# A decode step of attention and SwiGLU on one core: the output in two column tiles, the chain ahead of W_O on two engines, W_O in five pieces

## The chip, the cores and the metric

The kernel runs on one core of one Trainium2 chip. The metric is the device time of one execution in microseconds, on the slowest core, which here is the only one. Five engines work side by side, each with its own program: TensorE (PE in the profile) for matmuls, VectorE (DVE), ScalarE (ACT), GpSimd (POOL) and SyncE (SP), which mostly issues DMAs. They wait for each other on semaphores. Matmuls write into PSUM, and DVE and ACT read it from there.

## The reference

One new token for each of four sequences (B = 4, D = 512). The normed input goes through grouped-query attention over the last 4096 positions of a cache (32 query heads, 8 key/value heads of 128), and beside it through a SwiGLU feed-forward of width 1792. Cut to what matters:

```python
xn = layernorm(x)                                   # (4, 1, 512)
q  = xn @ wq                                        # 32 heads of 128
p  = softmax(q . k[:, :, Sk-4096:] * 128 ** -0.5)   # k, v: 8 heads, each for 4 query heads
a  = concat_heads(p . v) @ wo                       # wo: 4096 x 512
f  = (silu(xn @ w_gate) * (xn @ w_up)) @ w_down     # 1792 wide
return x + a + f
```

All inputs and the output are bf16. The windows of the two caches are 32 MB each, the weights another 13 MB.

## The kernel before, in words

**Loads.** SP (`on_sync`) issues nearly all loads, in one order: Wq, W_gate, W_up, then for each key/value head g = 0 to 7 the whole K of that head (4 MB, into `KB[g % 2]`) and the whole V (4 MB, into `VB[g % 2]`), then W_down, then W_O. The K load of head g waits until the transposes of head g-2 are done (L242), the V load until the products with V of head g-2 are done (L253). W_O goes into the buffer of K of head 6, so it waits for that head's transposes (L265). It comes in four pieces of 22, 5, 3 and 2 rows of 1 KB per partition (`WOS`); W_O's 4096 rows of 512 lie as 32 rows `e` on 128 partitions, and each piece has its own semaphore. At the end SP stores the left half of the output.

**One group per head** (the loop at L500, two heads a turn because of the two buffers). K arrives with positions on partitions and must be transposed: 16 chunks `c` of 8 transposes (`transposes`, L417), three PSUM banks `ps_kt` in turn. Each chunk is evicted into `KT`, by ACT for the chunks in `ACT_CH` (L281) and by DVE for the others (L330). Two chunks later `scores` (L432) multiplies them with the queries into four banks `ps_S`. DVE takes maxima (L336), PE and DVE turn them into one shift per query (L338 to L345), PE adds the shift (L444), ACT takes the exponential (L284) and `pv` (L453) multiplies by V into the left half of `ps_O`; sums of the exponentials (L459) go into the right half of the same bank. DVE then copies the left half to `Osb` (L348) and sums the right half into `dsum` (L349), one after the other. `fin` (L466, L468), run inside the next head's loop after its third chunk, finishes both sums, and DVE's `norm` (L353 to L358) divides and writes `OT`. `warm` puts matmuls of no use (`spin`, L474) into gaps of PE: five before the maxima, five before the shift, and four after `pv` of each even head from head 2 on.

**The end.** After the last head: `fin`, `down` (the feed-forward's last product, 14 matmuls into `acc4_ps`, L478), four small matmuls that bring `OT` into the order that W_O wants (L524, into one bank `perm_ps`), one DVE copy into `OP` (L374). Then PE takes W_O's pieces as they land. The first `WOE` = 22 rows go through `acc4`: 512 columns wide, one row `e` on each of four column tiles of 32 in turn, so that four partial sums stand in `acc4_ps`. ACT copies these to `S2` (L292), and a product with `sel4` adds them up. That product is in PE's program behind the second piece. The remaining rows go through `acc`: four matmuls per row, one for each 128 output columns, each on a column tile of its own, into `acc_ps`. So the four quarters of the output stand on four groups of partitions. DVE copies two of them into `y` (L377), ACT the other two (L295), SP stores the left half (L269) and ACT the right half (L298), and SP waits for both.

Of the kernel before, what the change touches and what calls it, by code (L numbers as in the profile page):

```python
# [10 lines left out]
def bass_parallel_sum__sliding_block_cached__swiglu_ffn__decode_kernel(  # L11
# [25 lines left out]
    NT = W // NJ  # L37
# [6 lines left out]
    SCALE = float(Dh) ** -0.5  # L44
    EPS = 1e-5
    OFF = -1.0e9
    WOS = (0, 22, 27, 30, 32)
    WOE = 22
    NR = HQ * Dh // 128

    def sb(name, shape, dtype, align=32):
# [65 lines left out]
    O_ps = ps_O[:, 0:2 * Dh]  # L117
    O2_ps = ps_S[3][:, 0:NH]
    D2_ps = ps_S[3][:, 64:64 + NH]
    den_ps = ps_O[:, 256:512]  # L120
    DT = 256 // NH
    q_ps = ps_S[0][:, 0:HQ * B]
    gate_ps = ps_O[:, 64:64 + NF * B]
    up_ps = ps_O[:, 128:128 + NF * B]
    xT_ps = ps_S[2][:, 0:NC * B]
    HD = D // 4
    acc_ps = ps_S[0][:, 0:HD]
    acc4_ps = ps_S[1]
    perm_ps = ps_kt[2][:, 0:B * NR]

    def sem(name):
        return nc.alloc_semaphore(name=name)
# [3 lines left out]
    d_wu = sem("d_wu")  # L136
    d_wd = sem("d_wd")
    d_out = sem("d_out")
    d_wo = [sem("d_wo%d" % q) for q in range(4)]
# [23 lines left out]
    s_p = sem("s_p")  # L163
    s_pv = sem("s_pv")
    s_dn = sem("s_dn")
    s_fin = sem("s_fin")
    s_nrm = sem("s_nrm")
    s_pm = sem("s_pm")
# [1 line left out]
    s_e = sem("s_e")  # L170
    s_ec = sem("s_ec")
    s_acc = sem("s_acc")
    s_y = [sem("s_y%d" % n) for n in range(2)]

    x_ap = A_x.rearrange("b s d -> (b s) d")
    out_ap = out.rearrange("b s (n c) -> n (b s) c", n=2)
# [61 lines left out]
    def on_sync(eng):  # L238
        def load(g):
            u = g % 2  # L240
            if g >= 2:
                eng.wait_ge(s_tr, NCH * (g - 1))  # L242
            if g < HKV - 1:
                eng.dma_start(KB[u][:], kv_ap(A_k_cache, g, 0, NT)).then_inc(d_k[u], 16)
            else:

                H = NT // 2
                eng.dma_start(KB[u][:, 0:H], kv_ap(A_k_cache, g, 0, H)).then_inc(d_k[u], 16)
                eng.dma_start(KB[u][:, H:], kv_ap(A_k_cache, g, H, NT)).then_inc(d_kh, 16)
            if g == 1:  # L250
                eng.wait_ge(s_q, 1)
            if g >= 2:
                eng.wait_ge(s_pv, g - 1)  # L253
            eng.dma_start(VB[u], kv_ap(A_v_cache, g, 0, NT)).then_inc(d_v[u], 16)

        def load_wo(n, a, b):
            eng.dma_start(WO[:, a:b, :], wo_ap[:, a:b, :]).then_inc(d_wo[n], 16)  # L257
# [11 lines left out]
        eng.dma_start(out_ap[0], y[:, 0:D // 2]).then_inc(d_out, 16)  # L269
        eng.wait_ge(d_out, 32)  # L270

    def on_scalar(eng):
        eng.wait_ge(s_go, 1)
        eng.dma_start(X[:], x_ap).then_inc(d_x, 16)
        eng.wait_ge(s_var, 1)
        eng.activation(st_std[:], st_var[:], ACT.Sqrt).then_inc(s_std, 1)

        def group(r):
            for n, c in enumerate(ACT_CH):
                eng.wait_ge(s_tr, r * NCH + (c + 1))  # L280
                eng.activation(KT[:, c % 4], kt_ps[c % 3], ACT.Copy).then_inc(s_ea, 1)  # L281
# [10 lines left out]
        eng.activation(S2[:], acc4_ps[:], ACT.Copy).then_inc(s_ec, 1)  # L292
        eng.wait_ge(s_acc, 1)
        for n in range(2, 4):
            last = eng.activation(y[:, HD * n:HD * (n + 1)], acc_ps[32 * n:32 * n + B, :], ACT.Copy)  # L295
        last.then_inc(s_y[1], 1)
        eng.wait_ge(s_y[1], 1)
        eng.dma_start(out_ap[1], y[:, D // 2:D]).then_inc(d_out, 16)  # L298

    def on_vector(eng):  # L300
        eng.wait_ge(d_x, 16)
# [24 lines left out]
        def group(r, rest=None):  # L326
            for c in range(NCH):
                if c not in ACT_CH:
                    eng.wait_ge(s_tr, r * NCH + (c + 1))
                    eng.tensor_copy(KT[:, c % 4], kt_ps[c % 3]).then_inc(s_ev, 1)  # L330
                if c == 2 and rest:
                    rest()
                for q in range(NB):
                    if c == min(NCH - 1, (q + 1) * NCH // NB + 1):
                        eng.wait_ge(s_sc, r * NB + (q + 1))
                        eng.tensor_reduce(mx[:, q, :], ps_S[q][:].rearrange("p (t n) -> p n t", n=NH), AX.X, ALU.max)  # L336
            eng.drain()
            eng.tensor_reduce(m16[:], mx[:].rearrange("p q n -> p n q"), AX.X, ALU.max).then_inc(s_m, 1)  # L338
            eng.tensor_copy(QC[:], QT[:, r + 1] if isinstance(r, int) else QT[:, bass.ds(r + 1, 1)].rearrange("p o n -> p (o n)"))
# [5 lines left out]
            eng.scalar_tensor_tensor(CM[0:NH, :], neg[:], M[:, 0:1], coff[:], ALU.mult, ALU.add).then_inc(s_cm, 1)  # L345

            eng.wait_ge(s_pv, r + 1)
            eng.tensor_copy(Osb[:], O_ps)  # L348
            eng.tensor_reduce(dsum[:], den_ps.rearrange("p (t n) -> p n t", n=NH), AX.X, ALU.add).then_inc(s_dn, 1)  # L349

        def norm(r):
# [19 lines left out]
            group(r, lambda: norm(r - 1))  # L371
        norm(HKV - 1)
        eng.wait_ge(s_pm, 1)
        eng.tensor_copy(OP[:, :, 0:B].rearrange("p r b -> p b r"), perm_ps.rearrange("p (b r) -> p b r", b=B)).then_inc(s_pc, 1)  # L374
        eng.wait_ge(s_acc, 1)
        for n in range(2):
            last = eng.tensor_copy(y[:, HD * n:HD * (n + 1)], acc_ps[32 * n:32 * n + B, :])  # L377
        last.then_inc(s_y[0], 1)

    def on_tensor(eng):  # L380
        mm = eng.matmul
# [22 lines left out]
        eng.sem_inc(s_p, NB)  # L404
        eng.sem_inc(s_nrm, 1)
        eng.sem_inc(s_dn, 1)
        eng.wait_ge(s_zero, 1)
        eng.wait_ge(s_guT, 1)

        def transposes(r, u, c):  # L410
            if c == 0:
                eng.wait_ge(d_k[u], (r - u) * 8 + 16)
            if u and c == NCH // 2:
                with eng.If(r > HKV - 2):
                    eng.wait_ge(d_kh, 16)
            for k in range(CH):
                last = eng.transpose(kt_ps[c % 3][:, k, :], KB[u][:, CH * c + k, :], ident[:])  # L417
            last.then_inc(s_tr, 1)
# [29 lines left out]
        def pv(r, u):  # L448
            for t in range(0, NT, 2):
# [6 lines left out]
                if t % DT == DT - 2:  # L456
                    e = t // DT
                    n = e % 4
                    last = mm(den_ps[32 * n:32 * n + 32, :], ones[:, 0:32],  # L459
                              P[:, DT * e:DT * (e + 1), :].rearrange("p t n -> p (t n)"),  # L460
                              start=False, stop=(e >= NT // DT - 4), skip_group_check=True)
            last.then_inc(s_pv, 1)

        def fin(r):
            eng.wait_ge(s_dn, r + 1)
            mm(D2_ps, head[:], dsum[:], start=True, stop=True, skip_group_check=True)  # L466
            for h in range(2):
                last = mm(O2_ps, Osb[:, Dh * h:Dh * (h + 1)], sel[:, NH * h:NH * (h + 1)],  # L468
                          start=(h == 0), stop=(h == 1), skip_group_check=True)
# [8 lines left out]
            return mm(acc4_ps[32 * n:32 * n + 32, :], left, right, start=start, stop=stop, skip_group_check=True)  # L478

        def acc(left, right, start, stop):  # L480
            for n in range(4):
                last = mm(acc_ps[32 * n:32 * n + B, :], left, right[:, HD * n:HD * (n + 1)],
                          start=start, stop=stop, skip_group_check=True)
            return last
# [4 lines left out]
            for t in range(NF):  # L489
                acc4(t % 4, guT[:, t, :], WD[:, t, :], t < 4, False)  # L490

        def warm(r, u, n):

            if u:
                spin(n)
            else:
                with eng.If(r > 0):
                    spin(n)

        with eng.Fori(0, HKV, 2) as r0:  # L500
            for u in range(2):
# [13 lines left out]
                eng.wait_ge(d_v[u], (r - u) * 8 + 16)  # L515
                pv(r, u)
                if u == 0:
                    warm(r, u, 4)

        fin(HKV)  # L520
        down()
        eng.wait_ge(s_nrm, HKV + 1)
        for b in range(B):
            last = mm(perm_ps[:, NR * b:NR * (b + 1)], OT[:, b].rearrange("p k h q -> p (k h q)"), dr[:])  # L524
# [4 lines left out]
        for q in range(4):  # L529
            eng.wait_ge(d_wo[q], 16)  # L530
            for e in range(WOS[q], WOS[q + 1]):
                if e < WOE:
# [45 lines left out]
```

## Time and profile before

| | us |
|---|---|
| time, median of 3 runs | 195.56 (195.43 to 195.69) |
| the profiled execution's own time | 195.57 |
| its span, first to last instruction | 194.2 |
| PE busy / DVE busy / ACT busy | 158.9 / 103.5 / 61.6 |
| mean granted clock of PE | 0.991 |

The profile's page gives busy times per engine, the span in 40 equal slices (one digit each, the busy tenths), the DMA queues, the chain of work that ended last, and the costliest groups of instructions: line, engine, operation, output <- inputs, shape, count, busy us, mean ns of one, and idle time before them. The other views used are the chain in order of time (start, us, what), the timeline (start, us, engine, line, operation) and a table by stretches of time: busy us and count of PE, PE's weight loads, DVE, ACT and POOL, then the granted clock of PE, the busy share of the 16 DMA engines and GB/s. Matmuls are pipelined and their ends are modelled, so their times overlap.

### The profile page before, as it was taken

The page shows a single profiled execution, that of the slowest core. Times are in us where ns is not written, and L with a number is a line of the kernel's source. Part 1 is how long each engine was busy: PE and PEld are TensorE (multiplying, and loading weights), DVE is VectorE, ACT ScalarE, POOL GpSimd, SP SyncE. Part 2 cuts the span into 40 slices and gives each one's busy share as a digit, 9 for nine tenths or more (in the row PEclk, how much of TensorE's full clock was granted, in tenths as well). Part 3 has the DMA queues.
Part 4 walks back from the last instruction along what each step waited for, and adds up shares of the span by engine and source line. Part 5 has one row for each costly group of instructions (what it writes and reads, how often), then busy time and mean ns, then how long its engine had stood idle before and what let it go on. Part 6 is the DMA issues. An engine that isn't in the chain of part 4 may idle for free.

```text
span 194.2 us, 7226 instructions
## 1 busy us (share of the span) xinstructions
PE 158.9 (82%) x3138; PEld 131.4 (68%) x3138; DVE 103.5 (53%) x218; ACT 61.6 (32%) x79; POOL 10.2 (5%) x49
## 2 busy tenths in 40 slices
PE   0009843998699899999999899989996999999964
PEld 0009843997388849966994699459945984897531
DVE  0071020368256837871886389338933893678241
ACT  1020000243405442624451345314531553063402
POOL 8750000000000000000000000000000000000000
PEclk9999999999789999999999999999999999999999
DMA  6999999999999999999999999999999999999992
GB/s 216 433 436 428 430 429 432 432 429 432 429 439 430 422 429 459 432 432 439 432 439 432 432 432 439 432 439 432 432 432 432 432 402 432 462 439 399 440 398 104
DMA packets 3634, 81.16 MB, mean 418 GB/s; under 512 B 412, under 2 KB 424, under 8 KB 808
## 3 DMA queue, kind: packets, MB, share of 16 engines
q1 hardware_dynamic: 3608, 81.01, 97.3%
q8 instruction: 8, 0.13, 0.2%
q14 instruction: 2, 0.02, 0.0%
q10 hardware_dynamic: 16, 0.01, 0.0%
HBM read 81.01 MB, written 0.00 MB: 417 GB/s over the span
## 4 chain that ended last, share of the span: by engine, by line
DMA 59%; PE 35%; DVE 3%; SPq 1%; issue 1%; DVEq 0%
DMA kbuf<-in_A_k_cache_dram 43%; PE ps_kt L417 21%; DMA kbuf<-in_A_wo_dram 16%; PE ps_s L432 7%; PE ps_o L453 3%; PE ps_s L468 1%; PE ps_kt L474 1%; PE ps_s L444 1%; DVE kT L330 1%; DVE mx L336 1%; SPq L257 1%; PE ps_s L466 1%; PE ps_o L459 0%; DVE y_sb L377 0%; PE ps_kt L439 0%
## 5 line engine op out<-in xcount | busy, mean ns | idle before, releaser
L417 PE MATMUL ps_kt<-ident,kbuf 128*128 128x128 bf16 x1024 | 78.4, 224 | 10.2 <-DMA kbuf<-in_A_k_cache_dram 9.8
L417 PEld LDWEIGHTS ps_kt<-ident,kbuf 128*128 128x128 bf16 x1024 | 60.7, 100 | 12.2 <-DMA kbuf<-in_A_k_cache_dram 10.9
L330 DVE COPY kT<-ps_kt 128x1024 bf16<-128x1024 bf16 x88 | 57.7, 686 | 20.4 <-PE ps_kt L417 19.6
L281 ACT ACTIVATE kT<-ps_kt 128x1024 bf16<-128x1024 bf16 x40 | 41.0, 1024 | 65.4 <-PE ps_kt L417 65.4
L432 PE MATMUL ps_s<-qC,kT 128*128 128x16 bf16 x1024 | 44.9, 170 | 2.9 <-DVE kT L330 2.0
L432 PEld LDWEIGHTS ps_s<-qC,kT 128*128 128x128 bf16 x1024 | 38.0, 97 | 4.8 <-DVE kT L330 4.0
L284 ACT ACTIVATE p<-ps_s 128x512 bf16<-128x512 f32 x32 | 16.5, 602 | 34.3 <-PE ps_s L444 34.3
L336 DVE TENSOR_REDUCE mx<-ps_s 128x16 f32<-128x512 f32 x32 | 22.0, 689 | 6.2 <-PE ps_s L432 4.2
L474 PE MATMUL ps_kt<-own,ones 128*128 128x512 bf16 x84 | 21.2, 380 | 0.0
L453 PE MATMUL ps_o<-vbuf,p 128*32 128x256 bf16 x512 | 19.2, 290 | 0.3
L453 PEld LDWEIGHTS ps_o<-vbuf,p 128*32 128x32 bf16 x512 | 15.0, 102 | 6.0 <-ACT p L284 4.2
L348 DVE COPY osb<-ps_o 128x256 f32<-128x256 f32 x8 | 3.4, 425 | 28.7 <-PE ps_o L459 28.7
L459 PE MATMUL ps_o<-p,ones 128*32 128x256 bf16 x64 | 16.9, 288 | 0.0
L385 PE MATMUL ps_s<-i,xn 4*128 4x4 f32 x4 | 0.6, 254 | 14.5 <-DVE xn L316 14.5
L474 PEld LDWEIGHTS ps_kt<-own,ones 128*128 128x128 bf16 x84 | 6.8, 97 | 6.8 <-issue 0.6
L385 PEld LDWEIGHTS ps_s<-i,xn 4*128 4x128 f32 x4 | 0.5, 207 | 14.4 <-issue 14.4
L444 PE MATMUL ps_s<-cm,own 128*128 128x512 bf16 x32 | 8.3, 380 | 1.0 <-DVE cm L345 1.0
L459 PEld LDWEIGHTS ps_o<-p,ones 128*32 128x32 bf16 x64 | 6.6, 103 | 0.1
L302 DVE TENSOR_REDUCE st_sum<-x_sb 4x1 f32<-4x512 bf16 x1 | 0.7, 674 | 10.2 <-DMA x_sb<-in_A_x_dram 10.2
L444 PEld LDWEIGHTS ps_s<-cm,own 128*128 128x128 bf16 x32 | 2.5, 97 | 5.3 <-DVE cm L345 3.4
L468 PE MATMUL ps_s<-sel,osb 128*128 128x16 f32 x36 | 5.8, 275 | 0.0
L468 PEld LDWEIGHTS ps_s<-sel,osb 128*128 128x128 f32 x36 | 5.2, 208 | 0.0
(85 smaller groups left out, 76.1 us busy)
## 6 DMA issues: line engine op xcount, KB each, us to landing
vbuf<-in_A_v_cache_dram SPq DMA_DIRECT2D x8, 4096.0 KB, 30.3
kbuf<-in_A_k_cache_dram SPq DMA_DIRECT2D x7, 4096.0 KB, 27.0
vbuf<-in_A_wq_dram SPq DMA_DIRECT2D x1, 4096.0 KB, 12.1
kbuf<-in_A_k_cache_dram SPq DMA_DIRECT2D x2, 2048.0 KB, 25.3
kbuf<-in_A_wo_dram SPq DMA_DIRECT2D x1, 2816.0 KB, 29.4
wg_sb<-in_B_w_gate_dram SPq DMA_DIRECT2D x1, 1792.0 KB, 16.2
wu_sb<-in_B_w_up_dram SPq DMA_DIRECT2D x1, 1792.0 KB, 21.1
wd_sb<-in_B_w_down_dram SPq DMA_DIRECT2D x1, 1792.0 KB, 34.5
```

The costliest lines, as they stand in the source:

```text
L281: eng.activation(KT[:, c % 4], kt_ps[c % 3], ACT.Copy).then_inc(s_ea, 1)
L284: eng.activation(P[:, BT * q:BT * (q + 1), :], ps_S[q][:].rearrange("p (t n) -> p t n", n=NH), ACT.Exp, scale=SCALE).then_inc(s_p, 1)
L330: eng.tensor_copy(KT[:, c % 4], kt_ps[c % 3]).then_inc(s_ev, 1)
L336: eng.tensor_reduce(mx[:, q, :], ps_S[q][:].rearrange("p (t n) -> p n t", n=NH), AX.X, ALU.max)
L348: eng.tensor_copy(Osb[:], O_ps)
L417: last = eng.transpose(kt_ps[c % 3][:, k, :], KB[u][:, CH * c + k, :], ident[:])
L432: last = mm(ps_S[q][:, NH * t:NH * (t + 1)], KT[:, c % 4, k, :], QC[:], start=(t == 0), stop=False, skip_group_check=True)
L444: mm(ps_S[q][:].rearrange("p (t n) -> p t n", n=NH), own[:], CM[:].unsqueeze(1).to_broadcast([128, BT, NH]), start=False, stop=True, skip_ ...
L453: mm(O_ps[32 * n:32 * n + 32, :], P[:, t:t + 2, :].rearrange("p t n -> p (t n)"), VB[u][:, t:t + 2, :].rearrange("p t d -> p (t d)"), star ...
L459: last = mm(den_ps[32 * n:32 * n + 32, :], ones[:, 0:32], P[:, DT * e:DT * (e + 1), :].rearrange("p t n -> p (t n)"), start=False, stop=(e ...
L468: last = mm(O2_ps, Osb[:, Dh * h:Dh * (h + 1)], sel[:, NH * h:NH * (h + 1)], start=(h == 0), stop=(h == 1), skip_group_check=True)
L474: mm(ps_kt[k][:], ones[:], own[:].unsqueeze(1).to_broadcast([128, 4, 128]), skip_group_check=True)
```

## The change

- **Output in two column tiles.** `HD` is 256 instead of 128: `acc` issues two matmuls of 256 columns per row instead of four of 128. DVE copies the left half of the output in one instruction, ACT the right half in one. One store of the whole output goes out from ACT, which waits for both copies (`s_y` at 2); SP no longer stores.
- **The chain ahead of W_O on two engines.** The sums of exponentials go to another bank (`ps_kt[2]` instead of the right half of `ps_O`), the copy to `Osb` moves from DVE to ACT (with the new semaphore `s_os`), and DVE does only the sum `dsum`. This holds for every head. Because chunk 2 of the next head uses `ps_kt[2]`, its transposes now wait for `dsum`. The reordered heads go to two banks, and DVE and ACT each copy half into `OP`. The four spins after `pv` write to another bank and are left out ahead of the last head too.
- **W_O in five pieces** of 16, 8, 5, 2 and 1 rows; `WOE` is 16, and the product with `sel4` comes straight after the first piece.

```diff
-    WOS = (0, 22, 27, 30, 32)
-    WOE = 22
+    WOS = (0, 16, 24, 29, 31, 32)
+    WOE = 16
-    den_ps = ps_O[:, 256:512]
+    den_ps = ps_kt[2][:, 0:256]
-    HD = D // 4
+    HD = D // 2
-    perm_ps = ps_kt[2][:, 0:B * NR]
+    perm_ps = [ps_kt[h][:, 0:B // 2 * NR] for h in (2, 0)]
...
     # on_sync
-        eng.wait_ge(s_y[0], 1)
-        eng.dma_start(out_ap[0], y[:, 0:D // 2]).then_inc(d_out, 16)
-        eng.wait_ge(d_out, 32)
+        eng.wait_ge(d_out, 16)
...
     # on_scalar, end of each group
+            eng.wait_ge(s_pv, r + 1)
+            eng.activation(Osb[:], O_ps, ACT.Copy).then_inc(s_os, 1)
...
     # on_scalar, the end
+        eng.wait_ge(s_pm, 1)
+        eng.activation(OP[:, :, 2:B].rearrange("p r b -> p b r"),
+                       perm_ps[1].rearrange("p (b r) -> p b r", b=2), ACT.Copy).then_inc(s_pc, 1)
         eng.wait_ge(s_e, 1)
         eng.activation(S2[:], acc4_ps[:], ACT.Copy).then_inc(s_ec, 1)
         eng.wait_ge(s_acc, 1)
-        for n in range(2, 4):
-            last = eng.activation(y[:, HD * n:HD * (n + 1)], acc_ps[32 * n:32 * n + B, :], ACT.Copy)
-        last.then_inc(s_y[1], 1)
-        eng.wait_ge(s_y[1], 1)
-        eng.dma_start(out_ap[1], y[:, D // 2:D]).then_inc(d_out, 16)
+        eng.activation(y[:, HD:D], acc_ps[32:32 + B, :], ACT.Copy).then_inc(s_y, 1)
+        eng.wait_ge(s_y, 2)
+        eng.dma_start(out_ap, y[:]).then_inc(d_out, 16)
...
     # on_vector
             eng.wait_ge(s_pv, r + 1)
-            eng.tensor_copy(Osb[:], O_ps)
             eng.tensor_reduce(dsum[:], ...).then_inc(s_dn, 1)
...
-        eng.tensor_copy(OP[:, :, 0:B].rearrange("p r b -> p b r"), ...).then_inc(s_pc, 1)
+        eng.tensor_copy(OP[:, :, 0:2].rearrange("p r b -> p b r"), ...).then_inc(s_pc, 1)
         eng.wait_ge(s_acc, 1)
-        for n in range(2):
-            last = eng.tensor_copy(y[:, HD * n:HD * (n + 1)], acc_ps[32 * n:32 * n + B, :])
-        last.then_inc(s_y[0], 1)
+        eng.tensor_copy(y[:, 0:HD], acc_ps[0:B, :]).then_inc(s_y, 1)
...
     # on_tensor
         def transposes(r, u, c):
+            if c == 2:
+                eng.wait_ge(s_dn, r + 1)
...
         def fin(r):
             eng.wait_ge(s_dn, r + 1)
             mm(D2_ps, head[:], dsum[:], start=True, stop=True, skip_group_check=True)
+            eng.wait_ge(s_os, r + 1)
...
         def acc(left, right, start, stop):
-            for n in range(4):
+            for n in range(2):
...
                 if u == 0:
-                    warm(r, u, 4)
+                    with eng.If(r < HKV - 2):
+                        warm(r, u, 4, 1)
...
-        eng.wait_ge(s_pc, 1)
-        for q in range(4):
+        eng.wait_ge(s_pc, 2)
+        for q in range(len(WOS) - 1):
...
             if WOS[q + 1] == WOE:
                 last.then_inc(s_e, 1)
-            if q == 1:
                 eng.wait_ge(s_ec, 1)
                 acc(sel4[:], S2[:], False, False)
```

More of the change, by code (lines that the diff above doesn't have):

```diff
@@ L138, in bass_parallel_sum__sliding_block_cached__swiglu_ffn__decode_kernel @@
     d_out = sem("d_out")
-    d_wo = [sem("d_wo%d" % q) for q in range(4)]
+    d_wo = [sem("d_wo%d" % q) for q in range(len(WOS) - 1)]
     d_k = [sem("d_k%d" % s) for s in range(2)]
@@ L165, in bass_parallel_sum__sliding_block_cached__swiglu_ffn__decode_kernel @@
     s_dn = sem("s_dn")
+    s_os = sem("s_os")
     s_fin = sem("s_fin")
@@ L172, in bass_parallel_sum__sliding_block_cached__swiglu_ffn__decode_kernel @@
     s_acc = sem("s_acc")
-    s_y = [sem("s_y%d" % n) for n in range(2)]
+    s_y = sem("s_y")
     x_ap = A_x.rearrange("b s d -> (b s) d")
-    out_ap = out.rearrange("b s (n c) -> n (b s) c", n=2)
+    out_ap = out.rearrange("b s c -> (b s) c")
     wq_ap = A_wq.rearrange("(p c) n -> p c n", c=NC)
@@ L373, in on_vector @@
         eng.wait_ge(s_pm, 1)
-        eng.tensor_copy(OP[:, :, 0:B].rearrange("p r b -> p b r"), perm_ps.rearrange("p (b r) -> p b r", b=B)).then_inc(s_pc, 1)
+        eng.tensor_copy(OP[:, :, 0:2].rearrange("p r b -> p b r"),
+                        perm_ps[0].rearrange("p (b r) -> p b r", b=2)).then_inc(s_pc, 1)
         eng.wait_ge(s_acc, 1)
-        for n in range(2):
-            last = eng.tensor_copy(y[:, HD * n:HD * (n + 1)], acc_ps[32 * n:32 * n + B, :])
-        last.then_inc(s_y[0], 1)
+        eng.tensor_copy(y[:, 0:HD], acc_ps[0:B, :]).then_inc(s_y, 1)
     def on_tensor(eng):
@@ L406, in on_tensor @@
         eng.sem_inc(s_dn, 1)
+        eng.sem_inc(s_os, 1)
         eng.wait_ge(s_zero, 1)
@@ L460, in pv @@
                               P[:, DT * e:DT * (e + 1), :].rearrange("p t n -> p (t n)"),
-                              start=False, stop=(e >= NT // DT - 4), skip_group_check=True)
+                              start=(e < 4), stop=(e >= NT // DT - 4), skip_group_check=True)
             last.then_inc(s_pv, 1)
@@ L490, in down, with warm @@
                 acc4(t % 4, guT[:, t, :], WD[:, t, :], t < 4, False)
-        def warm(r, u, n):
+        def warm(r, u, n, k=2):
             if u:
-                spin(n)
+                spin(n, k)
             else:
                 with eng.If(r > 0):
-                    spin(n)
+                    spin(n, k)
         with eng.Fori(0, HKV, 2) as r0:
@@ L523, in on_tensor @@
         for b in range(B):
-            last = mm(perm_ps[:, NR * b:NR * (b + 1)], OT[:, b].rearrange("p k h q -> p (k h q)"), dr[:])
+            last = mm(perm_ps[b // 2][:, NR * (b % 2):NR * (b % 2 + 1)], OT[:, b].rearrange("p k h q -> p (k h q)"), dr[:])
         last.then_inc(s_pm, 1)
@@ L527, in on_tensor @@
         acc(ident[0:B, 0:B], X[:], True, False)
-        eng.wait_ge(s_pc, 1)
-        for q in range(4):
+        eng.wait_ge(s_pc, 2)
+        for q in range(len(WOS) - 1):
             eng.wait_ge(d_wo[q], 16)
```

## The prediction

> **What bounds the kernel now.** I read the page's busy shares, the DMA row and the chain that ended last, then the chain's last stretch, then the DMA share in fine slices at the end.
>
> ```profile
> span 194.2 us, 7226 instructions
> PE 158.9 (82%) x3138; PEld 131.4 (68%) x3138; DVE 103.5 (53%) x218; ACT 61.6 (32%) x79; POOL 10.2 (5%) x49
> DMA  6999999999999999999999999999999999999992
> q1 hardware_dynamic: 3608, 81.01, 97.3%
> DMA 59%; PE 35%; DVE 3%; SPq 1%; issue 1%; DVEq 0%
> ```
>
> The DMA row is at nine tenths or more from the second slice to the last but one: 81 MB pass at the engines' pace, and neither PE (82%) nor DVE (53%) sets it. The 35% of PE in the chain are transposes that release the issue of a load which then lies in the queue; W_O was issued at 159.35 and its first piece landed 29.4 us later (rows below). So I look only at what stands after the last byte, and at whether work beside the stream becomes longer than the stream.
>
> ```profile
> 160.67 31.17 DMA kbuf<-in_A_wo_dram
> 191.85 0.04 issue
> 191.89 0.31 PE ps_s L482 x8
> 192.20 0.02 issue
> 192.23 0.28 DVE y_sb L377
> 192.50 0.01 issue
> 192.52 0.28 DVE y_sb L377
> 192.22 0.55 ACT L295 ACTIVATE y_sb<-ps_s 4x128 bf16<-4x128 f32 x2 [1.22 <-PE ps_s L482]
> 192.81 0.27 ACTq L298 DMA_DIRECT2D out_dram<-y_sb  x1
> 192.83 0.35 SPq L269 DMA_DIRECT2D out_dram<-y_sb  x1
> 193.56:193.60 0.04, 0.00 (x0) 0.00 (x0) 0.00 (x0) 0.00 (x0) 0.00 (x0) 1.00 0.09 26
> 193.72:193.76 0.04, 0.00 (x0) 0.00 (x0) 0.00 (x0) 0.00 (x0) 0.00 (x0) 1.00 0.07 13
> ```
>
> This is the whole uncovered tail: landing 191.85, eight matmuls to 192.20, two copies on each engine to 192.80, two store issues, store bytes from 193.56 to 193.76, end at 194.2. Together 2.35 us, or 1.2% of the span; no step here can give more than a part of that.
>
> The rest of the working uses these rows: issues and landings of W_O, the work ahead of it, and the last group's start.
>
> ```profile
> 159.35 1.76 SPq L257 DMA_DIRECT2D kbuf<-in_A_wo_dram  x4
> 159.72 0.43 SPq L257
> 160.20 0.43 SPq L257
> kbuf<-in_A_k_cache_dram SPq DMA_DIRECT2D x7, 4096.0 KB, 27.0
> kbuf<-in_A_wo_dram SPq DMA_DIRECT2D x1, 2816.0 KB, 29.4
> kbuf<-in_A_wo_dram SPq DMA_DIRECT2D x1, 640.0 KB, 30.6
> kbuf<-in_A_wo_dram SPq DMA_DIRECT2D x1, 384.0 KB, 31.0
> kbuf<-in_A_wo_dram SPq DMA_DIRECT2D x1, 256.0 KB, 31.2
> 166.11 1.04 PE L474 MATMUL ps_kt<-own,ones 128*128 128x512 bf16 x4
> 166.99 1.50 PE L417 MATMUL ps_kt<-ident,kbuf 128*128 128x128 bf16 x24
> 184.62 0.42 DVE L348 COPY osb<-ps_o 128x256 f32<-128x256 f32 x1 [3.38 <-PE ps_o L459]
> 184.96 0.41 DVE L349 TENSOR_REDUCE dsum<-ps_o 128x16 f32<-128x256 f32 x1
> 187.47 0.72 DVE L374 CAST oP<-ps_kt 128x128 bf16<-128x128 f32 x1 [0.36 <-PE ps_kt L524]
> 188.90 1.47 PE L478 MATMUL ps_s<-kbuf,oP 128*32 128x512 bf16 x22 [0.86 <-DMA kbuf<-in_A_wo_dram]
> 190.41 0.60 ACT L292 ACTIVATE s<-ps_s 128x512 f32<-128x512 f32 x1 [6.62 <-PE ps_s L478]
> 191.06 0.40 PE L482 MATMUL ps_s<-s,sel 128*4 128x128 f32 x8 [0.26 <-ACT s L292]
> L453 PE MATMUL ps_o<-vbuf,p 128*32 128x256 bf16 x512 | 19.2, 290 | 0.3
> L444 PE MATMUL ps_s<-cm,own 128*128 128x512 bf16 x32 | 8.3, 380 | 1.0 <-DVE cm L345 1.0
> L339 DVE COPY qC<-qT 128x16 bf16 x7 | 1.1, 161 | 0.0
> ```
>
> Issue plus landing time puts the pieces at 188.75, 190.32, 191.20 and 191.85. The gaps are 1.57 us for five rows, 0.88 for three, 0.65 for two: about 0.31 us a row.
>
> **The change, part by part.** The terms on the path first.
>
> *Last matmuls.* Eight matmuls of 128 columns (0.31 us) become two of 256. One of 256 columns lasts 0.290 (L453); the second starts 0.01 to 0.05 behind it, so 0.30 to 0.34. Range -0.01 to +0.03; I take 0.
>
> *Output copies.* DVE: two of 0.28 become one of 256 columns. The f32 copy of 256 columns (L348) takes 0.42, and a cast of 128 already takes 0.28, so I take 0.41. ACT: 0.27 for 128 columns and 0.60 for 512 (L292) put 256 near 0.38, so DVE ends last. 0.57 becomes 0.41: -0.16.
>
> *One store.* ACT now waits for both copies (s_y at 2) and nothing is queued behind the store on it. 192.23 + 0.41 + 0.04 (the gap that ACT shows today) = 192.68, where its store starts today at 192.81: -0.13, which already contains the copies' gain. Then SP's store, today issued 0.02 later and 0.08 longer in issue, is gone. The bytes of both stores lie between 193.56 and 193.76: if SP's is the second, up to 0.19 more goes; if ACT's is, none does. The issue times say SP's, so I take 0.07 more, near the difference in issue. Copies and store together: -0.20, bounds -0.13 and -0.32.
>
> *A fifth W_O piece.* The bytes stay, so the last landing moves only by what a piece costs beside its bytes. Two rows took 0.65; the step from two rows to three took 0.23, and five against three (1.57 - 0.88)/2 = 0.345 a row. 0.65 less two rows is thus -0.04 to 0.19. The long piece is the steadier measure, so I take +0.05. SP's extra issue (0.43 + 0.04) ends near 161.2, more than 20 us before those bytes are due, and SP then only waits for the output.
> [...]
>
> Sum: 0 - 0.20 + 0.05 = -0.15 on the profiled execution's 195.57 (its span 194.2 and 1.37 around it): 195.42. The median of the runs is 195.56, so I say 195.4. The bounds add up to 195.20 and 195.66.
>
> Now the parts that I cost at nothing, and what covers them.
>
> *Osb to ACT, denominators to another bank.* Eight copies of 0.42 leave DVE, eight of some 0.39 (between ACT's two sizes above) go onto ACT. The sum dsum starts at once, 0.34 sooner. On ACT the copy waits for pv; behind it are the next group's evictions, the first of which needs the fourth chunk. PE's transposes of the third chunk now wait for dsum: behind that wait stand fin and all scores. dsum ends about 0.5 after pv, and chunks one and two take 16/24 of 1.50, 1.0 us, so PE should not stop. If it did, the stream would still hold the time: SP's next load of K waits for transposes, but such a load lands 27.0 after its issue while its own 4 MB take about 10 at the pace of 81 MB in 191 us, so some 17 us lie ahead of it in the queue.
>
> *Four spins gone ahead of the last group.* They took 1.04 us at 166.11, and the transposes began at 166.99. K of that group was there, since PE took it without a wait; so the last group starts up to 0.9 sooner. That moves no load.
>
> *Chain to W_O.* OP stands at 188.19 today. -0.34 from dsum; the eviction of 128 columns splits: (0.72 - 0.16)/2 + 0.16 = 0.44 on DVE with L339 as the least price, 0.28 less. On ACT such a stepped write is not shown; 0.22 to 0.72 bounds it, and I take 0.44, since DVE's row is the same pattern. OP at 187.57, or near 186.7 with the earlier last group. The first piece, six rows shorter, lands near 188.75 - 6 x 0.305 = 186.92.
>
> *The wait on S2 moves ahead of 16 rows.* From 187.57: 16 matmuls of 512 columns, of which 22 take 1.47 and one 0.38 (L444), so a step of 0.052 and 15 x 0.052 + 0.38 = 1.16; ACT's copy 0.60 and three hand-overs of 0.05; the sum over S2, some 0.25 of issue (0.40 less one matmul's 0.27, doubled because two column tiles share the work of four); then 15 rows at 0.104 (512 columns step 0.052 with four tiles at work, so 0.208 in one tile, and half of that for 256). Ready for the last row at 191.29; it lands at 191.9. Some 0.6 us of cover, and over one if the last group is early.
>
> **Rivals.**
>
> *PE late (slower).* Place: PE at s_ec with all 16 late rows behind it. It decides once OP is later than about 188.2, today's own value, and costs over 0.2% (0.39 us, with the 0.15 gained to be lost first) from about 188.7 on. Against: OP should be earlier. For: the clock can fall.
>
> ```profile
> 48.00:49.00 1.00, 0.00 (x0) 0.00 (x0) 0.93 (x3) 0.00 (x0) 0.00 (x0) 1.00 1.06 459
> 52.00:53.00 1.00, 1.00 (x24) 0.78 (x20) 0.00 (x0) 0.80 (x2) 0.00 (x0) 0.50 1.24 524
> 189.00:190.00 1.00, 1.00 (x22) 0.49 (x17) 0.00 (x0) 0.00 (x0) 0.00 (x0) 1.00 0.96 377
> ```
>
> After a sparse stretch the granted clock stood at 0.50 at 52 us, while the tail ran at 1.00. At half clock from the first piece on, the 1.16 would be about 2.1, the S2 sum 0.5 and 15 rows 3.1: with copy and hand-overs 6.45 after 187.0, thus 193.45 against 191.9. That gives 195.4 + 1.5 = 196.9. Chance 1 in 10, all of it slower.
> [...]
>
> *Pieces have a floor.* If no piece lands faster than the 0.65 seen for two rows, one row costs 0.3 more than I took: 195.7. Against: two rows are already near two rows' share. On top of the forecast's high bound it gives 195.96, just over 0.2%. 1 in 10, of which 2 in 100 there.
>
> *The stores hinder each other (faster).* Both go out at once and the end comes 0.4 us after the last bytes. If the second also delays the first's completion, one store saves the full 0.32 and perhaps half of that 0.4: about -0.5, 195.1. For: the bytes come in two bursts. Against: 0.4 may be pure delay. 2 in 10.
>
> **How the numbers follow.** My forecast has 6 in 10, PE late 1, floor 1, hindering stores 2. Under 0.2% (0.39 us) is about what cannot be told from no change here; the forecast and most of the floor lie within it. Faster: 0.20 plus 0.02 of the forecast's edge. Slower: 0.10 + 0.02. Same: 0.66. The range 195.05 to 195.85 leaves out PE late and the lower part of the stores' case; the forecast's own is 195.20 to 195.66.
>
> **What would show it.** Right: the last W_O landing within 0.2 us of 191.85; one DVE copy near 0.41; ACT's store issued about 0.8 us after the landing and the end 1.3 after that; PE idle ahead of each of the last pieces. Wrong: PE not waiting for W_O at the end, a granted clock below 1.00 after 186 us, or a last landing later by half a microsecond.

## The result, and the profile after

The changed kernel takes 195.32 us (median of 22 runs, 195.10 to 195.61), the kernel before 195.59 (22 runs, 195.42 to 195.82). The ratio is 0.9986, with a 95% interval of 0.9980 to 0.9993: faster by 0.27 us. That is under the 0.2% that I had set as the limit of what can be told, but the interval does not reach 1, so it can be told. A second measurement on another occasion gave 195.28 against 195.62 (0.9983, 0.9974 to 0.9992). The forecast was 195.4.

The page of the changed kernel, lines as shown of before:

```profile
span 194.3 us, 7189 instructions
PE 160.9 (83%) x3114; PEld 131.5 (68%) x3114; DVE 100.6 (52%) x209; ACT 65.0 (33%) x87; POOL 10.0 (5%) x49
DMA  6999999999999999999999999999999999999992
q1 hardware_dynamic: 3744, 81.00, 97.3%
```

DVE gave up 2.9 us of work and ACT took 3.4; the DMA row is the same from end to end. The span of this one execution is even a little longer than before. It is the slowest of the 22 runs (195.61): the last row of W_O reaches PE at 192.29 in it, where a second trace of the same kernel (195.36) has it at 192.06. What the change did is therefore read from the last landing on. First the chain's end, then the waits of PE's weight loads, the store's issue and the slices with the store's bytes:

```profile
160.58 30.73 DMA kbuf<-in_A_wo_dram
191.31 0.04 issue
191.35 1.23 PE ps_s L487 x16
192.59 0.02 issue
192.61 0.41 DVE y_sb L379
191.96 0.09 PEld L487 LDWEIGHTS ps_s<-kbuf,oP 128*4 128x4 bf16 x4 [0.18 <-DMA kbuf<-in_A_wo_dram]
192.29 0.08 PEld L487 LDWEIGHTS ps_s<-kbuf,oP 128*4 128x4 bf16 x2 [0.25 <-DMA kbuf<-in_A_wo_dram]
193.05 0.27 ACTq L301 DMA_DIRECT2D out_dram<-y_sb  x1
193.80:193.84 0.04, 0.00 (x0) 0.00 (x0) 0.00 (x0) 0.00 (x0) 0.00 (x0) 1.00 0.07 26
193.92:193.96 0.04, 0.00 (x0) 0.00 (x0) 0.00 (x0) 0.00 (x0) 0.00 (x0) 1.00 0.08 26
```

The last three pieces reach PE at 191.35, 191.96 and 192.29: 0.61 us for two rows and 0.33 for one, so the small pieces come in proportion to their rows. The last row's matmuls take 0.30 (192.29 to 192.59), the copy 0.41, and the store's bytes pass from 193.80 to about 193.97. From the last matmul to the end of the span it is 1.7 us, where before it was 2.0. That is the gain; its steps are set side by side below, behind the parts.

The work ahead of W_O, from the timeline of DVE, ACT and PE:

```profile
184.15 0.42 DVE L351 TENSOR_REDUCE dsum<-ps_kt 128x16 f32<-128x256 f32 x1 [3.38 <-PE ps_kt L463]
184.15 0.38 ACT L286 ACTIVATE osb<-ps_o 128x256 f32<-128x256 f32 x1 [0.83 <-PE ps_kt L463]
186.67 0.43 DVE L376 CAST oP<-ps_kt 128x64 bf16<-128x64 f32 x1 [0.36 <-PE ps_kt L530]
186.67 0.45 ACT L294 ACTIVATE oP<-ps_kt 128x64 bf16<-128x64 f32 x1 [2.14 <-PE ps_kt L530]
187.41 1.05 PE L483 MATMUL ps_s<-kbuf,oP 128*32 128x512 bf16 x16
189.15 0.60 PE L487 MATMUL ps_s<-s,sel 128*4 128x256 f32 x4 [0.70 <-ACT s L297]
```

OP stands at 187.12, 1.07 us sooner than before, and the first piece of W_O, now of 16 rows, is there almost at once: PE begins at 187.41, where it began at 188.90.

### The profile page after: what moved, and what is told of

It reads as the page before. It is cut to its first block, busy times and chain, and to the rows that moved or that the text cites. A ratio compares the mean times of both kernels' runs of the same rounds, so it can differ in the third digit from the quotient of the medians.

```text
span 194.3 us, 7189 instructions
## 1 busy us (share of the span) xinstructions
PE 160.9 (83%) x3114; PEld 131.5 (68%) x3114; DVE 100.6 (52%) x209; ACT 65.0 (33%) x87; POOL 10.0 (5%) x49
## 3 DMA queue, kind: packets, MB, share of 16 engines
q1 hardware_dynamic: 3744, 81.00, 97.3%
## 4 chain that ended last, share of the span: by engine, by line
PE 48%; DMA 44%; DVE 3%; issue 3%; SPq 1%; DVEq 0%
DMA kbuf<-in_A_k_cache_dram 29%; PE ps_kt L421 24%; DMA kbuf<-in_A_wo_dram 16%; PE ps_s L436 8%; PE ps_kt L479 5%; PE ps_o L457 5%; PE ps_s L448 2%; DVE kT L333 2%; PE ps_s L473 2%; PE ps_s L470 1%; PE ps_s L487 1%; PE ps_kt L463 1%; PE ps_kt L443 0%; DVE mx L339 0%; SPq L258 0%
## 5 line engine op out<-in xcount | busy, mean ns | idle before, releaser
L351 DVE TENSOR_REDUCE dsum<-ps_kt 128x16 f32<-128x256 f32 x8 | 3.4, 425 | 30.1 <-PE ps_kt L463 30.1
L463 PE MATMUL ps_kt<-p,ones 128*32 128x256 bf16 x64 | 17.1, 291 | 0.0
L448 PE MATMUL ps_s<-cm,own 128*128 128x512 bf16 x32 | 9.1, 411 | 1.0 <-DVE cm L348 1.0
L463 PEld LDWEIGHTS ps_kt<-p,ones 128*32 128x32 bf16 x64 | 6.6, 103 | 0.1
L286 ACT ACTIVATE osb<-ps_o 128x256 f32<-128x256 f32 x8 | 3.1, 384 | 9.0 <-PE ps_kt L463 9.0
```

Of the source, the lines that this page charges most:

```text
L448: mm(ps_S[q][:].rearrange("p (t n) -> p t n", n=NH), own[:], CM[:].unsqueeze(1).to_broadcast([128, BT, NH]), start=False, stop=True, skip_ ...
L463: last = mm(den_ps[32 * n:32 * n + 32, :], ones[:, 0:32], P[:, DT * e:DT * (e + 1), :].rearrange("p t n -> p (t n)"), start=(e < 4), stop= ...
```

## The experiments

Each was timed in five rounds beside the kernel before, except where told. `OUT` below stands for the output part of the diff (two tiles, one copy per engine, one store), `CHAIN` for the split chain with the spins and the moved bank, `PIECES` for the five pieces with `WOE = 16` and the product with `sel4` straight after the first.

| kernel | median us | range of runs | kernel before, same occasion | ratio, 95% interval |
|---|---|---|---|---|
| output part alone | 195.36 | 195.23 to 195.71 | 195.65 | 0.9983 (0.9967 to 0.9999) |
| pieces alone | 195.59 | 195.45 to 195.82 | 195.65 | 0.9992 (0.9977 to 1.0008) |
| chain alone | 195.80 | 195.42 to 196.83 | 195.65 | 1.0009 (0.9988 to 1.0029) |
| changed, two stores | 195.52 | 195.25 to 195.86 | 195.65 | 0.9990 (0.9973 to 1.0006) |
| output and chain | 195.57 | 195.29 to 196.80 | 195.56 | 1.0014 (0.9996 to 1.0032) |
| output and pieces | 195.50 | 195.30 to 195.82 | 195.56 | 0.9995 (0.9986 to 1.0003) |
| chain and ten spins | 195.65 | 195.52 to 195.77 | 195.56 | 1.0003 (0.9994 to 1.0012) |
| changed, OP 1.2 us later | 195.43 | 195.16 to 197.00 | 195.56 | 0.9997 (0.9983 to 1.0012) |
| output part, last two rows 1 + 1 | 195.28 | 195.18 to 195.41 | 195.62 | 0.9984 (0.9975 to 0.9993) |
| the same, last row in 16 DMAs | 198.11 | 198.05 to 198.32 | 195.62 | 1.0129 (1.0114 to 1.0145) |
| changed, again | 195.28 | 195.18 to 195.52 | 195.62 | 0.9983 (0.9974 to 0.9992) |

### Each part alone

The output part alone, on the kernel before:

```diff
-    HD = D // 4
+    HD = D // 2
...
+        eng.activation(y[:, HD:D], acc_ps[32:32 + B, :], ACT.Copy).then_inc(s_y, 1)
+        eng.wait_ge(s_y, 2)
+        eng.dma_start(out_ap, y[:]).then_inc(d_out, 16)
```

> The output part alone: two column tiles, one copy per engine, one store; W_O in four pieces and the chain as before. Forecast's theory (the gain is the work behind the last landing, one copy of 0.41 in place of 0.57 and a store less): 0.20 us faster than before, or a little more since the whole change measured -0.27. Rival 'stores hinder each other': 0.4 to 0.5 faster. Rival 'the W_O pieces or the chain carry the gain': within 0.1 of before. In the profile: from the last matmul's end to the end of the span 1.7 us, where before it is 2.0.

Measured: 0.29 us faster, as much as the whole change by the medians; the interval reaches from 0.02 to 0.65 us. From its timeline:

```profile
191.84 0.38 PE L476 MATMUL ps_s<-kbuf,oP 128*4 128x256 bf16 x4
191.84 0.09 PEld L476 LDWEIGHTS ps_s<-kbuf,oP 128*4 128x4 bf16 x4 [0.27 <-DMA kbuf<-in_A_wo_dram]
192.27 0.41 DVE L372 CAST y_sb<-ps_s 4x256 bf16<-4x256 f32 x1 [4.12 <-PE ps_s L476]
192.71 0.27 ACTq L294 DMA_DIRECT2D out_dram<-y_sb  x1
```

The last matmul ends at 192.22 to 192.25, nearly where it did before (192.20), and the span at 194.0 instead of 194.2. The matmuls behind the last piece have become longer: here that piece still has two rows, and its four matmuls of 256 columns take 0.38 us, where eight of 128 took 0.31.

The pieces alone:

```diff
-    WOS = (0, 22, 27, 30, 32)
-    WOE = 22
+    WOS = (0, 16, 24, 29, 31, 32)
+    WOE = 16
...
-            if q == 1:
                 eng.wait_ge(s_ec, 1)
                 acc(sel4[:], S2[:], False, False)
```

> W_O in five pieces alone, with the sel4 product straight after the first; output end and chain as before. Forecast's theory: the bytes are the same and a further piece costs about 0.05, so 0 to 0.1 slower than before. Rival 'the pieces carry the gain': 0.2 faster. Rival 'pieces have a floor': 0.3 slower.

Measured: 0.06 faster, with an interval on both sides of none. Neither the floor of the rival (0.3 slower) nor a gain.

The chain alone:

```diff
-    den_ps = ps_O[:, 256:512]
+    den_ps = ps_kt[2][:, 0:256]
...
+            eng.wait_ge(s_pv, r + 1)
+            eng.activation(Osb[:], O_ps, ACT.Copy).then_inc(s_os, 1)
...
+                    with eng.If(r < HKV - 2):
+                        warm(r, u, 4, 1)
```

> The chain ahead of W_O split over DVE and ACT alone; output end and pieces as before. Forecast's theory: the first piece of W_O (22 rows) lands after OP is ready anyway, so within 0.1 us of before. Rival 'the chain carries the gain': 0.2 faster.

Measured: a median 0.15 above before, and a spread that no theory had: seven runs from 195.42 to 195.89, five from 196.06 to 196.83. The profiled one is among these (196.56). Its PE timeline, and two stretches of 3.41 us (the columns as before: PE, weight loads, DVE, ACT, POOL, then granted clock, DMA share, GB/s):

```profile
186.98 0.22 PE L492 MATMUL ps_s<-x_sb,ident 4*4 4x128 bf16 x4
189.18 1.08 PE L488 MATMUL ps_s<-kbuf,oP 128*32 128x512 bf16 x12 [1.98 <-DMA kbuf<-in_A_wo_dram]
186.21:189.62 3.41, 1.43 (x21) 0.58 (x23) 0.51 (x2) 0.45 (x1) 0.00 (x0) 1.00 0.91 373
189.62:193.03 3.41, 3.26 (x63) 2.08 (x58) 0.00 (x0) 0.60 (x1) 0.00 (x0) 0.50 0.33 129
```

With the chain a microsecond earlier and the first piece still of 22 rows, PE stands idle for 1.98 us. In this run the granted clock then falls to 0.50 at 189.62, just as W_O begins, and stays there until 193.03, while nearly all of W_O's matmuls run: PE, not the landing, decides the end. That the other four long runs had the same fall is likely from their times, but they have no trace.

The store undone, on the changed kernel:

```diff
     # on_sync
-        eng.wait_ge(d_out, 16)
+        eng.wait_ge(s_y, 1)
+        eng.dma_start(out_ap[:, 0:HD], y[:, 0:HD]).then_inc(d_out, 16)
+        eng.wait_ge(d_out, 32)
...
     # on_scalar
-        eng.wait_ge(s_y, 2)
-        eng.dma_start(out_ap, y[:]).then_inc(d_out, 16)
+        eng.wait_ge(s_y1, 1)
+        eng.dma_start(out_ap[:, HD:D], y[:, HD:D]).then_inc(d_out, 16)
```

> The changed kernel with the store of the output undone: each engine's half is stored by itself as before, ACT's by ACT and DVE's by SP, and SP waits for both. Forecast's theory: the single store was worth 0.07 beside the copies, so 0.05 to 0.1 slower than the changed kernel (0.2 faster than before). Rival 'stores hinder each other': 0.3 slower than the changed kernel, about as before.

Measured: 0.13 faster than before, where the changed kernel is 0.27 and 0.34 faster on other occasions. By the medians one store in place of two would be worth 0.14 to 0.21 us, but the interval of this kernel alone is some 0.3 us to either side; the traces below put it at 0.06 to 0.07. Its tail:

```profile
192.41 0.41 DVE L382 CAST y_sb<-ps_s 4x256 bf16<-4x256 f32 x1 [5.49 <-PE ps_s L490]
192.82 0.28 ACTq L304 DMA_DIRECT2D out_dram<-y_sb  x1
192.85 0.35 SPq L271 DMA_DIRECT2D out_dram<-y_sb  x1
```

### The tail in the traces, step by step

The medians above differ by little more than their noise. The steps behind the last row of W_O recur within 0.01 or 0.02 us in every trace that has them, so they tell the parts apart. The first column is the time at which PE loads the weights for the last piece; the others are lengths in us, the last step up to the end of the span (194.22, 194.01, 194.35, 194.22, 194.35, 194.11 and 193.99).

| kernel | last piece at PE | to the copies | copies to store issue | store issue to end | together |
|---|---|---|---|---|---|
| before | 191.89 | 0.34 | 0.58 | 1.41 | 2.33 |
| output part alone | 191.84 | 0.43 | 0.44 | 1.30 | 2.17 |
| pieces alone | 192.08 | 0.28 | 0.59 | 1.40 | 2.27 |
| changed, two stores | 192.10 | 0.31 | 0.41 | 1.40 | 2.12 |
| changed | 192.29 | 0.32 | 0.44 | 1.30 | 2.06 |
| changed, again | 192.06 | 0.32 | 0.44 | 1.29 | 2.05 |
| output part, last two rows 1 + 1 | 191.94 | 0.31 | 0.45 | 1.29 | 2.05 |

Beside the lines already shown, the table rests on these: two of the pieces alone, one of the two stores, two of the changed kernel again, two of the output part with one row more.

```profile
192.08 0.09 PEld L482 LDWEIGHTS ps_s<-kbuf,oP 128*4 128x4 bf16 x4 [0.23 <-DMA kbuf<-in_A_wo_dram]
192.95 0.27 ACTq L298 DMA_DIRECT2D out_dram<-y_sb  x1
192.10 0.08 PEld L490 LDWEIGHTS ps_s<-kbuf,oP 128*4 128x4 bf16 x2 [0.24 <-DMA kbuf<-in_A_wo_dram]
192.06 0.08 PEld L487 LDWEIGHTS ps_s<-kbuf,oP 128*4 128x4 bf16 x2 [0.23 <-DMA kbuf<-in_A_wo_dram]
192.82 0.27 ACTq L301 DMA_DIRECT2D out_dram<-y_sb  x1
191.94 0.08 PEld L476 LDWEIGHTS ps_s<-kbuf,oP 128*4 128x4 bf16 x2 [0.17 <-DMA kbuf<-in_A_wo_dram]
192.70 0.27 ACTq L294 DMA_DIRECT2D out_dram<-y_sb  x1
```

So the one copy per engine is worth 0.14 us. The single store is worth 0.11 counted from its issue, and 0.06 to 0.07 against the changed kernel with two stores, whose ACT can issue 0.03 sooner. Two column tiles make the matmuls of a last piece of two rows 0.09 longer, and a last piece of one row takes this back: the output part alone has 0.16 of the gain in its tail, and with the one-row piece 0.28. When the last row lands varies by more than any of these steps, from 191.84 to 192.29 here, so single traces don't show what a piece costs in landing time.

### The parts in pairs, and what holds the clock

Output and chain without the pieces (`OUT` and `CHAIN`; the edit is to the changed kernel):

```diff
-    WOS = (0, 16, 24, 29, 31, 32)
-    WOE = 16
+    WOS = (0, 22, 27, 30, 32)
+    WOE = 22
...
+            if q == 1:
                 eng.wait_ge(s_ec, 1)
                 acc(sel4[:], S2[:], False, False)
```

> The changed kernel with W_O in the old four pieces (22, 5, 3, 2) and the sel4 product behind the second: output part and chain part alone. The chain part alone showed a median 0.15 us above before with single runs up to 196.8, and its profiled run had a granted clock of 0.50 from 189.5 us on, after PE had stood 2 us ahead of the first piece. Theory 'clock': the earlier chain makes PE wait too long for a first piece of 22 rows; here too some runs lie 0.8 us and more above the others, which are at 195.3; the five pieces are what keeps PE busy. Rival 'the pieces only add a cost': all runs between 195.1 and 195.5.

Measured: seven runs from 195.29 to 195.68 and five from 196.16 to 196.80, a spread like that which the clock theory expects. The four longest have a mean clock of 0.983 where six of the others have 0.991, some 3 us more at half clock, worked out from the two means. The profiled run is the fifth (196.16), and its trouble lay elsewhere: the clock was 0.50 from 150 to 155 us and 0.81 from 155 to 160, and OP came at 189.64. So no trace of this kernel shows the fall ahead of W_O.

```profile
150.00:155.00 5.00, 5.00 (x70) 5.00 (x68) 2.75 (x7) 1.04 (x2) 0.00 (x0) 0.50 0.97 419
189.19 0.45 ACT L293 ACTIVATE oP<-ps_kt 128x64 bf16<-128x64 f32 x1 [2.14 <-PE ps_kt L529]
189.80 1.42 PE ps_s L482 x22
```

Output and pieces without the chain (`OUT` and `PIECES`; the edit is to the kernel before):

```diff
-    WOS = (0, 22, 27, 30, 32)
-    WOE = 22
+    WOS = (0, 16, 24, 29, 31, 32)
+    WOE = 16
...
-    HD = D // 4
+    HD = D // 2
...
-            if q == 1:
                 eng.wait_ge(s_ec, 1)
                 acc(sel4[:], S2[:], False, False)
```

> The changed kernel with the old chain: output part and five pieces alone. Forecast's theory: the chain costs and gives nothing by itself, so as the changed kernel, 0.25 us faster than before within 0.1, and no slow runs, since PE has its first piece at once when OP is ready. Rival 'the chain is needed for 16 rows behind S2': 0.2 us slower than the changed kernel or more.

Measured: 0.06 faster than before, which is some 0.2 short of the changed kernel, with no run above 195.82. The rival was right here: the chain is needed once 16 rows stand behind S2 with the output in two tiles. (The pieces alone, with four tiles of 128 columns, need it less: in their trace PE's last weight load still waits 0.23 us for its piece.) From the timeline of DVE and PE:

```profile
187.61 0.72 DVE L370 CAST oP<-ps_kt 128x128 bf16<-128x128 f32 x1 [0.36 <-PE ps_kt L518]
188.38 1.05 PE L472 MATMUL ps_s<-kbuf,oP 128*32 128x512 bf16 x16 [0.17 <-DVE oP L370]
190.13 0.60 PE L476 MATMUL ps_s<-s,sel 128*4 128x256 f32 x4 [0.70 <-ACT s L290]
190.56 1.92 PE L476 MATMUL ps_s<-kbuf,oP 128*4 128x256 bf16 x32
```

OP stands at 188.33, and from 190.56 PE runs through all 32 matmuls without a wait for DMA, to 192.48. In the changed kernel PE waits for the last pieces.

The chain alone again, with PE's gap filled (the edit is to the chain alone):

```diff
-        spin(2, 1)
+        spin(10, 1)
```

> The chain part alone with ten spins in place of two ahead of W_O, which fill PE's 2 us of waiting. Theory 'clock': no run above 195.9, median within 0.1 of before, granted clock 1.00 to the end. Rival 'something else in the chain part is slow, not the wait': median and slow runs as without the spins (195.8, up to 196.8).

Measured: 195.52 to 195.77, none above 196, median 0.09 above before. The gap is down to 0.26 and the clock stays at 1.00:

```profile
188.85 1.47 PE L488 MATMUL ps_s<-kbuf,oP 128*32 128x512 bf16 x22 [0.26 <-DMA kbuf<-in_A_wo_dram]
190.00:191.00 1.00, 0.67 (x26) 0.26 (x20) 0.00 (x0) 0.60 (x1) 0.00 (x0) 1.00 0.62 245
```

Nothing else was changed against the chain alone, and no run of eleven is long, where five of twelve were with the chain alone and five of twelve, on this same occasion, with output and chain. So PE's idle stretch ahead of W_O is what put most of those runs above 196.

The cover of the changed kernel, by holding OP back:

```diff
         eng.wait_ge(s_pm, 1)
+        for n in range(2):
+            eng.activation(pad[:, n]..., ones[:]..., ACT.Copy)   # 128x512 each
         eng.activation(OP[:, :, 2:B]..., ACT.Copy).then_inc(s_pc, 1)
```

> The changed kernel with two more ACT copies of 512 columns (0.6 us each) ahead of ACT's half of OP, into a buffer that nothing reads, so that OP is 1.2 us later. From the profile OP stands at 187.1 and PE would be ready for the last row 3.7 later, at 190.8, where it lands near 191.9: a cover of 1.1 us. Theory: as the changed kernel or up to 0.15 slower. If the cover is only the 0.6 worked out before the result: 0.6 slower. If the longer wait of PE lets the clock fall: single runs 1 us and more slower.

Measured: median 195.43, eleven runs from 195.16 to 195.66, one at 197.00. ACT's half of OP ends at 188.16 in its profile:

```profile
187.73 0.43 ACT L297 ACTIVATE oP<-ps_kt 128x64 bf16<-128x64 f32 x1
189.96 2.61 PE ps_s L490 x36
192.28 0.09 PEld L490 LDWEIGHTS ps_s<-kbuf,oP 128*4 128x4 bf16 x2 [0.25 <-DMA kbuf<-in_A_wo_dram]
```

PE's matmuls follow each other without a gap from 189.96 to 192.57, yet the weight load for the last piece still waits for the landing. So with OP held back by 1.04 us PE comes just in time, and 188.16 is about where the cover ends. The median is 0.14 to 0.21 short of the changed kernel's gain, which the noise of the two doesn't tell from nothing. The single run at 197.00 has a mean clock of 0.983, like the four longest runs of output and chain; that its clock fell at the same place is possible, but that run has no trace, and the kernel before has one run of 35 at 197.40 on another occasion.

### Towards a faster one

The output part alone, with one small piece more, so that nothing but the piece changes:

```diff
-    WOS = (0, 22, 27, 30, 32)
+    WOS = (0, 22, 27, 30, 31, 32)
```

> The output part alone, with the old chain, and the last W_O piece of two rows cut into one and one (22, 5, 3, 1, 1); the sel4 product stays behind the second piece, so PE is not the bound. It prices one more small piece where nothing else changes. Forecast's theory: +0.05 for the piece and about -0.05 for two matmuls fewer behind the landing: as the output part alone (0.29 us faster than before), within 0.1. Rival 'pieces have a floor': 0.3 slower than that, as before.

Measured: 195.28, 0.34 below before; the output part alone was 0.29 below. The further piece costs nothing that shows: by the traces the last piece's shorter matmuls take 0.12 us off the tail, and the medians show 0.05 of it, within their noise.

The same (the output part with the further piece) with the last row in 16 DMAs of 8 partitions, to shift bytes to those DMA engines that finish early:

```diff
+            if b == NR:
+                for p in range(0, 128, 8):
+                    eng.dma_start(WO[p:p + 8, a:b, :], wo_ap[p:p + 8, a:b, :]).then_inc(d_wo[n], 16)
+                return
...
-            eng.wait_ge(d_wo[q], 16)
+            eng.wait_ge(d_wo[q], 256 if WOS[q + 1] == NR else 16)
```

> The same, but the last row is issued as 16 DMAs of 8 partitions each instead of one of 128. Before, the DMA share falls from 0.96 to about 0.6 near 190 us and to nothing at 191.5: some engines are done 1.5 us ahead of the others. If a DMA of 8 partitions runs on 8 of the 16 engines, and these are the early ones, the late ones have 0.3 us less to do: 0.2 to 0.3 faster than the one-row version. If they are the late ones, 0.3 slower. If it is spread over all, the same. SP needs some 7 us for the issues, more than 20 us ahead of the bytes.

Measured: 198.11 (one round, four runs), 2.5 us slower than before, by a way that none of the expectations had. SP's issues of the 16 DMAs, the chain's end, and the stretches in which the bytes run out:

```profile
161.13 17.77 SPq L259 DMA_DIRECT2D kbuf<-in_A_wo_dram  x16
177.88 16.84 DMA kbuf<-in_A_wo_dram
194.71 0.04 issue
194.76 0.40 PE ps_s L480 x2
191.60:192.00 0.40, 0.40 (x8) 0.08 (x2) 0.00 (x0) 0.00 (x0) 0.00 (x0) 1.00 0.13 13
192.00:192.40 0.40, 0.00 (x0) 0.00 (x0) 0.00 (x0) 0.00 (x0) 0.00 (x0) 1.00 0.00 0
```

The bytes are through at about 192, but the last of the 16 DMAs counts as landed only at 194.71. That is 2.7 us behind the bytes. The page counts 112 packets more than with the last row in one DMA (3856 against 3744 in the queue of the loads), all of them under 512 B (536 against 424). Why the landing trails, and which engines the DMAs ran on, the trace does not tell, so the question behind the experiment stays open. The issues took 17.77 us where 7 were expected, and ended at 178.90, some 13 us before the bytes were through.

> The changed kernel again, beside the two others on one chip. Its median was 0.27 us below before; expected 0.2 to 0.35 below, no run more than 0.4 above its median. Theory 'the output part is the whole gain': within 0.1 of the one-row version.

Measured: 195.28, the same as the output part with one more row piece. Nothing that was tried beats the changed kernel.

## Why the prediction was right, step by step

**The time.** Forecast 195.4 (-0.15), measured 195.32 (-0.27), inside the forecast's own range of 195.20 to 195.66 and within 0.2% as said. The sign and the place are right: the gain is behind the last landing.

**The steps behind the landing.** The tail is 2.06 us (2.05 in the second trace) where it was 2.33: -0.27, the whole of what was measured. The forecast had the right steps, and each came out a little better than taken:

- *Last matmuls:* -0.02, taken as 0. This needs the last piece to be one row; with two rows the two column tiles cost 0.09.
- *Copies, up to the store's issue:* -0.14, taken as -0.13. One copy lasts 0.41 on DVE, as worked out, and 0.38 on ACT.
- *SP's store gone:* -0.11 from the issue on, taken as -0.07. The 0.08 by which SP's issue is longer was the nearer row. The bound of 0.19, which lets the bytes of a second store go away, was not: the bytes pass in 0.17 us now and in 0.20 before, since the one store moves the same bytes.
- *The fifth piece:* +0.05 taken, nothing seen.

The forecast of -0.15 is 0.12 short because four small differences point the same way; that the median and the tail agree to the hundredth is luck, as the landings scatter by more.

**The fifth piece** costs nothing that shows, but it isn't priced either: pieces alone came to -0.06, and the output part with one row more gained 0.05 on the output part, both within the noise and both with the shorter matmuls of one row in them. One row came 0.33 us behind two rows: no floor at the 0.65 seen for two.

**The parts costed at nothing** do cost nothing together, but not each by itself, and there the forecast said too little. That the chain's 1.07 us gain nothing is right; I named W_O's landing as the cover. Its size was right too: the last group ends 0.47 sooner (up to 0.9 allowed), `dsum` starts 0.34 sooner within it and the copies into `OP` are 0.27 shorter (0.34 and 0.28 taken). But a chain that is early in front of a late first piece leaves PE idle for 2 us, and then five of twelve runs are long; in the one of them that has a trace the clock had fallen to 0.50. And with the output in two tiles the five pieces behind S2 need OP before about 188.2, which only the new chain gives. The two parts pay for each other: the output part with a last piece of one row, without the new chain and without a first piece of 16 rows, has the same median as the whole change.

**The rival "PE late"** had both mechanisms with their numbers. Its point of decision, OP at 188.2, lies between the two experiments: at 188.33 PE was late, at 188.16 it came just in time. Its price for half clock, 1.5 us, is a little above the 0.6 to 1.4 between the runs of the chain alone above 196 and its shortest, 195.42. Its chance of 1 in 10 fits the changed kernel, whose longest gap of PE behind OP is 0.70 us (22 and 11 runs, none above 195.61), not its chain alone, with a gap of 1.98. And the length of a single gap does not tell when the clock falls: the clock of 0.50 that the prediction shows at 52 us began at 51.35, and in the 3.41 us ahead of that PE's idle stretches were only 1.11 and 1.03 us long.

**The rival "the stores hinder each other"** wanted 0.5 and fell. What it had in mind is there, but small: from the last byte to the end it is 0.38 us with one store, 0.46 with two.

**What was to be seen:** the DVE copy 0.41 (yes), the store 0.8 after the landing (192.25 to 193.05, yes), the end 1.3 behind it (193.05 to 194.3, yes), PE waiting ahead of the last pieces (yes), the granted clock 1.00 after 186 us (yes). The last landing was 0.4 later in the profiled execution, more than the 0.2 allowed, and 0.17 later in the kernel's second trace.

**One reading was loose.** Of PE's 35% in the chain that ended last, the transposes (L417) are 21%; the scores (L432, 7%), the products with V (L453, 3%) and smaller groups are the rest. No term rests on it.

## What to carry to other kernels

Where the DMA engines are full from end to end, as here (the loads' packets fill 97.3% of the 16 engines' span), only what stands behind the last byte was left to win: 0.14 us by one copy in place of two, about 0.1 by one store in place of two. Cut the last piece so small that the work behind it doesn't grow: in two column tiles, two rows made it 0.09 us longer, one row did not. A chain that is hidden behind a transfer is not free to become shorter: in the trace of the chain alone PE stood idle for 1.98 us, and W_O's matmuls then ran at a granted clock of 0.50 for 3.41 us. So shorten the chain and the first piece together (PE's gap ahead of the sum over S2 is then 0.70), or fill the gap (0.26 with ten spins); the clock stood at 1.00 while W_O's matmuls ran, in both. Look at all runs and not at the median alone: five of twelve above 196 moved that of the chain alone by only 0.15. And where the steps are as small as the noise of the medians, compare the same step in several traces.

## What the runs showed of the hardware that was not expected

In the trace of the chain alone the granted clock fell to 0.50 behind an idle stretch of PE of 1.98 us; with that stretch filled down to 0.26 it stayed at 1.00. The clock stood at 0.50 for 3.41 us, from 189.62 to 193.03; in as long a stretch ahead of the fall PE was busy for 1.43 us. In the kernel before, the fall at 51.35 is alike: PE busy for 1.26 of the 3.41 us ahead of it, with no idle stretch over 1.11 us, then half clock for the next 3.42.

```profile
47.94:51.35 3.41, 1.26 (x5) 0.39 (x5) 1.80 (x6) 0.62 (x2) 0.00 (x0) 1.00 0.95 408
51.35:54.77 3.42, 3.39 (x65) 2.51 (x68) 0.00 (x0) 1.45 (x3) 0.00 (x0) 0.50 0.98 422
```

Why only five of twelve runs of the chain alone are long, no run here shows.

Sixteen DMAs of 8 KB each, with all their bytes moved by about 192 us, were complete only at 194.71, while a single DMA of the same 128 KB, in the changed kernel, came 0.33 us behind the piece ahead of it.
